# Attention output in the model dimension's own order, and w_in read in rows of 128 partitions behind unit 0's v

## The chip, the cores and the metric

The kernel runs on one core of one Trainium2 chip. The metric is the device time of one execution in microseconds, as the median over several runs of the whole kernel; less is better.

## What is computed

Per batch and head a gated recurrence over 768 steps gives an attention output; the heads are laid side by side (8 heads of 48, 384 in all) and go through a two-layer block whose activation is a rational function.

```python
# q, k, v, f_logit: [4, 8, 768, 48]
f = 1 / (1 + exp(-f_logit))
for t in range(768):
    state = f[:, :, t, :, None] * state + k[:, :, t, :, None] * v[:, :, t, None, :]
    y[:, :, t] = q[:, :, t] @ state
x = y, heads side by side            # [3072, 384]
h = x @ w_in                         # [384, 2048]
P = a0 + a1*h + a2*h**2 + a3*h**3
Q = 1 + |b0| * |h| + |b1| * h**2
out = (P / (Q + 1e-6)) @ w_out       # [2048, 384]
```

## The kernel before

The work is cut into 12 units of 256 tokens: unit n is batch n mod 4 and chunk n div 4, so a state is handed on from unit n to unit n + 4. Within a unit the heads go in four pairs (index a), and the tokens in two blocks j of 128.

The order of every instruction is written out by hand in the string ORDER (lines 19 to 100). A loop at the end calls one small function for each step; each engine then takes its own steps in that order and waits only for data, for buffers and for PSUM slots. There are four PSUM slots; "@1" behind a step names its slot. A step therefore waits for everything that stands before it on its own engine, and for the last reader of its slot.

The steps that matter here:

- ld n f, k, q (line 190): loads of 384 KB (or halves of 192 KB) on SP's DMA queue, with three buffers for each of them. ld n v goes on POOL's queue, since it casts to bf16.
- wi m0 m1 (load_w_in, lines 193 to 200): w_in's columns m0*128 to m1*128, cast to bf16, on POOL's queue. The contracted dimension of 384 lies in three groups kk of 128 partitions. One transfer is issued for each kk, and partition 32a + e of group kk holds row 96a + 32kk + e. The order issues "wi 4 16" right behind unit 0's first loads, and "wi 0 4" later, with no wait before it on POOL.
- vm n x (line 349): POOL copies parts of v together for the heads' middle piece; it waits for v.
- ci: POOL makes the identity matrix that the transposes need; cu and cm make the triangular matrices and the mask.
- ef, ls, cs, A: ACT takes exp and log of the gate, PE sums it along time (cs), ACT takes exp of the sums (A). xa (DVE, line 296): products of q and k with A. T (PE, line 312) transposes them, Te copies them out, sc (PE, line 334) makes the scores, mk (DVE, line 342) masks them.
- yb and yi (line 355, through ymm): the attention output, from the scores and from the carried state. They write 32 columns of a pair's 96 at a time; piece kk of pair a goes to partitions 32a to 32a + 31 and to column block kk of the PSUM tile, which is why w_in has the row order above. ye (ACT, line 411) copies it to xT. sv and st renew the state.
- h n m0 m1 (PE, line 432): x times w_in, four blocks of 128 columns; hy (ACT) copies it out. h n 12 16 is each unit's first or one of its first; unit 0 takes 12 16, then 8 12, 4 8 and 0 4.
- sq, ab, u, ln, lz, zd, p1, p2, pm, ta, ex, gm: the rational function on DVE, ACT and PE, where zd and ta are accumulating transfers of 512 KB on POOL's queue. o (PE, line 539) multiplies by w_out, oe and so bring it out.

In PE's order, unit 0's y and unit 1's transpose T 1 stand ahead of unit 0's first h; yb 0 uses slot 1, which cs 1 used before it.

Of the kernel before, what the change touches and what calls it, by code (L numbers as in the profile page):

```python
# [17 lines left out]

ORDER = """
cz 0; ab_ b a; ld 0 f 2 4; ld 0 v; ld 0 f 0 2; cz 3; cu 1; ld 0 k 0 2; cz 1; cu 0; ld 0 q 2 4; fa  # L20
ld 0 q 0 2; wi 4 16; ef 0 2 4; ld 0 k 2 4; cz 2; ef 0 0 2; ls 0 0 2; fr; ls 0 2 4; cs 0 2 4 @1; vm 0 1
ld 1 f; cs 0 0 2 @0; ld 1 v; A 0 1 0 2; A 0 1 2 4; xa 0 1 0 2; A 0 0 2 4; vm 0 0; A 0 0 0 2; ci; xa 0 0 2 4
ld 1 k; xa 0 0 0 2; xa 0 1 2 4; T 0 0 2 @2; T 0 2 4 @1; Te 0 0 2; Te 0 2 4; sc 0 0 @2; ld 1 q; sv 0 0 @0
ef 1; cm; sc 0 1 @3; mk 0 0; ls 1; ae 0; cs 1 @1; ab_ a s; mk 0 1; A 1 1; st 0 0; A 1 0; xa 1 1; sv 0 1
yb 0 0 2 @1; ld 2 f; yi 0 1; xa 1 0; yb 0 2 4; ld 2 q; wi 0 4; ye 0 s; fb; T 1 @3; st 0 1; h 0 12 16 @0
# [83 lines left out]
def kernel(  # L109
# [12 lines left out]
    nc = tc.nc  # L122
    B, H, S, D = q.shape
    C = 128
    P = 128
    HP = H // 2
    DM = H * D
    d_ff = moe_w_in.shape[1]
    KD = DM // P
# [11 lines left out]
    ld = ctx.enter_context(tc.tile_pool(name="ld", bufs=3))  # L141
# [22 lines left out]
    w_in_sb = consts.tile([P, KD, d_ff], BF16, name="w_in_sb")  # L164
# [26 lines left out]
                      in_=src[s["b"], hh, t0:t0 + NT, :].rearrange("h (p i) d -> p h (i d)", i=2))  # L191

    def load_w_in(m0, m1):

        n = (m1 - m0) * P
        for kk in range(KD):
            nc.gpsimd.dma_start(out=w_in_sb[:, kk, m0 * P:m1 * P],
                                in_=bass.AP(tensor=moe_w_in.tensor,
                                            offset=moe_w_in.offset + 32 * kk * d_ff + m0 * P,
                                            ap=[[96 * d_ff, HP], [d_ff, 32], [1, n]]))  # L200

    def load_w_out(m0, m1):
        nc.gpsimd.dma_start(out=w_out_sb[:, m0:m1, :],
# [148 lines left out]
    PIECE = ((0, 0), (0, 1), (1, 1), (1, 2))  # L352

    def ymm(s, j, a, kk, lhsT, rhs):
        nc.tensor.matmul(s["y"][32 * a:32 * a + 32, j, kk * C:kk * C + C].rearrange("e (i t) -> e i t", i=2),  # L355
                         lhsT, rhs, start=(j, a) not in s["begun"], stop=True, skip_group_check=True)
        s["begun"].add((j, a))

    def y_open(s, sl):
        if "y" not in s:  # L360
# [3 lines left out]
    def yi(n, j, sl=None):  # L364
        s = unit(n)
        y_open(s, sl)
        for kk in range(KD):
            for a in range(HP):
                ymm(s, j, a, kk, s["st"][j][:, a, 32 * kk:32 * kk + 32], s["T"][:, 0, :, a, R * j:R * j + R])

    def yb(n, a0=0, a1=HP, sl=None):
        s = unit(n)
        y_open(s, sl)
        for i0 in range(2):
            for par, kk in PIECE:
                for a in range(a0, a1):
                    for j in range(UB):
                        r = slice(R * j, R * j + R)
                        if kk == 1:
                            w = s["vm"][r, i0, a, 16 * par:16 * par + 32]  # L380
                        else:
                            w = s["v"][r, 2 * a + par, i0, 16 * par:16 * par + 32]
                        ymm(s, j, a, kk, w,
                            s["scm", a // 2][r, 2 * par + a % 2, i0 * C:i0 * C + C].rearrange("s (i t) -> s i t", i=2))
# [171 lines left out]
    def behind(i, mark):  # L556
        tc.add_manual_dep(i.ins, marks[mark].ins.name,
                          mybir.DependencyInfo(mybir.DependencyClass.Sync, mybir.DependencyReason.DATA),
                          reason="begins behind it")

    steps = dict(ld=load, wi=load_w_in, wo=load_w_out, ab_=load_ab, cu=const_u, ci=const_i, cm=const_m,
                 cz=const_z, fa=coef_a, fb=coef_b, fr=coef_r, ef=ef, ls=ls, cs=cs, A=A, xa=xa, T=T, Te=Te,
                 sc=sc, mk=mk, vm=vm, yi=yi, yb=yb, sv=sv, ye=ye, ae=ae, st=st, h=h, hy=hy, sq=sq, ab=ab, u=u, ln=ln,
# [38 lines left out]
```

## Time and profile before

| | |
|---|---|
| Runs shown | 247.44, 248.99, 253.96 us (median 248.99) |
| Span of the profiled execution | 247.6 us; the page gives no other time of it |
| Busy, share of the span | PE 88%, DVE 83%, ACT 77%, POOL 26%, PE weight loads 61% |
| TensorE clock granted | full in all slices |
| DMA queues, share of 16 engines | POOL's 61.6%, SP's 33.2% |
| First matmul of h | 30.5 us |
| w_in | 6 issues, 13.1 to 16.3 us from issue to landing |

A timeline row reads: start, length, engine, line, operation, out<-in, shape and count, and in brackets how long the engine had idled before it and what ended that. A row of the chain that ended last has start, length and what the end hung on. A row of DMA issues has the tensor, the queue, the count, the size of one and the median us from issue to landing. Rows that begin with q0 or q1 give a queue's packets, MB and the share that they took of 16 engines in the window that was asked for.

### The profile page before, as it was taken

The numbers are of one execution on the slowest core, as the hardware profiler recorded it, in microseconds if no ns is written. First come the engines' busy times: TensorE is split into PE (matmuls) and PEld (weight loads), VectorE is DVE, ScalarE is ACT, GpSimd is POOL, SyncE is SP. The second block draws the span as 40 slices with busy tenths as digits, with TensorE's granted clock in tenths as the row PEclk, the third lists the DMA queues.
The fourth block names the chain that finished last, engine by engine and source line by source line (L and its number), as shares of the span: only waits on it lengthen the run. The fifth ranks groups of instructions, "written<-read, shape, count | busy, mean of one in ns | idle before, by whom it ended". The sixth has DMA issues, their size and how long they took to land.

```text
span 247.6 us, 7084 instructions
## 1 busy us (share of the span) xinstructions
PE 216.8 (88%) x3128; PEld 151.8 (61%) x3128; DVE 205.9 (83%) x232; ACT 190.4 (77%) x197; POOL 64.4 (26%) x94
## 2 busy tenths in 40 slices
PE   0307898979899998989999999999999999999990
PEld 0204676667557675756767776656866867664550
DVE  5217568999998969979979999999899898999630
ACT  3402376998995986996988998997965997799961
POOL 7421004233022400543042144202203311133200
PEclk9999999999999999999999999999999999999999
DMA  7999999995979899999896998799934996389954
GB/s 116 203 188 177 199 221 263 195 173 91 160 140 165 196 225 238 233 243 178 210 225 106 179 259 175 141 200 281 203 36 88 164 208 132 77 159 197 176 116 128
DMA packets 64206, 43.72 MB, mean 177 GB/s; under 512 B 53680, under 2 KB 59184, under 8 KB 64176
## 3 DMA queue, kind: packets, MB, share of 16 engines
q0 software_dynamic: 22944, 24.39, 61.6%
q1 hardware_dynamic: 41088, 18.88, 33.2%
q8 instruction: 24, 0.39, 0.6%
q14 instruction: 6, 0.05, 0.0%
q10 hardware_dynamic: 144, 0.00, 0.0%
HBM read 25.17 MB, written 4.72 MB: 121 GB/s over the span
## 4 chain that ended last, share of the span: by engine, by line
PE 64%; DMA 11%; ACT 11%; issue 7%; DVE 3%; SPq 2%; ACTq 0%; POOLq 0%
PE hp L432 21%; PE op L539 17%; DMA fn<-in_f_logit_dram 7%; PE y L355 7%; PE u L466 5%; PE tp L312 4%; DMA gall<-hy 4%; PE cs L282 3%; PE sc L334 3%; ACT lq L491 2%; PE sv L403 2%; ACT qi L499 2%; ACT hy L446 2%; ACT lq L477 2%; SPq L190 2%
## 5 line engine op out<-in xcount | busy, mean ns | idle before, releaser
L539 PE MATMUL op<-w_out_sb,gall 128*128 128x384 bf16 x384 | 69.4, 327 | 2.8 <-issue 1.0
L432 PE MATMUL hp<-xT,w_in_sb 128*128 128x256 bf16 x576 | 69.5, 274 | 1.1 <-ACT xT L411 0.9
L432 PEld LDWEIGHTS <-w_in_sb 128*128 128x128 bf16 x576 | 55.5, 98 | 12.0 <-issue 1.5
L446 ACT CAST hy<-hp 128x1024 bf16<-128x1024 f32 x48 | 47.9, 1017 | 11.4 <-PE hp L432 11.2
L539 PEld LDWEIGHTS <-gall 128*128 128x128 bf16 x384 | 35.7, 98 | 28.0 <-issue 2.8
L499 ACT ACTIVATE qi<-lq 128x2048 bf16<-128x2048 f32 x24 | 45.9, 1919 | 0.2
L522 POOL DMA_DIRECT2D gall<-hy x24 | 22.4, 962 | 72.4 <-DVE gall L518 24.5
L486 POOL DMA_DIRECT2D z<-h x12 | 13.2, 1099 | 76.8 <-DVE z L458 29.5
L342 DVE TENSOR_TENSOR scm<-sc,mask 128x1024 bf16<-128x1024 f32 x24 | 29.0, 1219 | 4.5 <-PE sc L334 4.3
L531 DVE TENSOR_TENSOR gall<-gall,qi 128x2048 bf16<-128x2048 bf16 x24 | 29.2, 1219 | 4.2 <-DMA gall<-hy 2.4
L450 DVE TENSOR_TENSOR h<-hy 128x2048 bf16<-128x2048 bf16 x24 | 29.1, 1217 | 0.4 <-ACT hy L446 0.4
L518 DVE TENSOR_TENSOR gall<-gall,h 128x2048 bf16<-128x2048 bf16 x24 | 28.9, 1217 | 0.0
L477 ACT ACTIVATE lq<-u 128x1024 f32<-128x1024 f32 x24 | 24.1, 1031 | 3.1 <-PE u L466 2.9
L291 ACT ACTIVATE A<-cs 128x768 f32<-128x768 f32 (+1 forms) x26 | 18.7, 767 | 6.0 <-PE cs L282 5.8
L491 ACT ACTIVATE lq<-z 128x2048 f32<-128x2048 bf16 x12 | 23.1, 1921 | 0.0
L296 DVE TENSOR_TENSOR qkp<-kn,A 128x768 bf16<-128x768 f32 (+1 forms) x13 | 11.7, 900 | 13.2 <-DMA kn<-in_k_dram 7.9
L267 ACT ACTIVATE fn<-fn 128x768 f32<-128x768 f32 (+1 forms) x13 | 10.3, 799 | 15.7 <-DMA fn<-in_f_logit_dram 15.7
L312 PE MATMUL tp<-ident,qkp 128*128 128x128 bf16 x192 | 14.6, 235 | 8.3 <-DVE qkp L296 5.6
L282 PE MATMUL cs<-lsp,Ui 128*128 128x384 bf16 (+1 forms) x39 | 10.9, 346 | 9.3 <-ACT lsp L272 9.3
L320 DVE COPY qkT<-tp 128x2048 bf16<-128x2048 bf16 (+1 forms) x13 | 14.8, 1138 | 5.1 <-PE tp L312 3.0
L312 PEld LDWEIGHTS <-qkp 128*128 128x128 bf16 x192 | 12.5, 105 | 10.1 <-DVE qkp L296 7.5
L349 POOL COPY vmp<-vn 128x128 bf16<-128x128 bf16 x24 | 12.6, 603 | 18.0 <-DMA vn<-in_v_dram 18.0
(63 smaller groups left out, 286.3 us busy)
## 6 DMA issues: line engine op xcount, KB each, us to landing
gall<-hy POOLq DMA_DIRECT2D x24, 512.0 KB, 6.7
z<-h POOLq DMA_DIRECT2D x12, 512.0 KB, 6.5
out_dram<-osb SPq DMA_DIRECT2D x24, 192.0 KB, 4.1
fn<-in_f_logit_dram SPq DMA_DIRECT2D x11, 384.0 KB, 10.3
kn<-in_k_dram SPq DMA_DIRECT2D x11, 384.0 KB, 6.1
qn<-in_q_dram SPq DMA_DIRECT2D x11, 384.0 KB, 8.1
vn<-in_v_dram POOLq DMA_DIRECT2D x12, 192.0 KB, 8.6
w_out_sb<-in_moe_w_out_dram POOLq DMA_DIRECT2D x4, 384.0 KB, 9.7
```

What stands on the lines that cost most here:

```text
L312: nc.tensor.transpose(t[:, x, i, p, :], s["qk"][:, x, i, 2 * p:2 * p + 2, :].rearrange("t h d -> t (h d)"), ident)
L342: return nc.vector.tensor_mul(t, s["sc", g].rearrange("s r a i t -> s (r a) (i t)"), mb)
L432: nc.tensor.matmul(t[:, m - m0, :].rearrange("f (j t) -> f j t", j=UB), w_in_sb[:, kk, m * P:(m + 1) * P], s["x"][:, :, kk, :], start=(kk ...
L446: nc.scalar.copy(fl(big(s, "hy", "hy", 3), m0, m1), fl(s["hp", m0], 0, m1 - m0))
L450: return nc.vector.tensor_mul(fl(big(s, "h2", "h2", 2), m0, m1), fl(s["hy"], m0, m1), fl(s["hy"], m0, m1))
L477: nc.scalar.activation(fl(lq(s, g), m0 - 8 * g, m1 - 8 * g), fl(s["u", m0], 0, m1 - m0), AF.Ln, scale=regs[2], bias=1.0 + 1e-6)
L491: nc.scalar.activation(fl(lq(s, g), m0 - 8 * g, m1 - 8 * g), fl(s["z"], m0, m1), AF.Ln, scale=regs[2], bias=1.0 + 1e-6)
L499: nc.scalar.activation(fl(s["qi", g], m0 - 8 * g, m1 - 8 * g), fl(s["lq", g], m0 - 8 * g, m1 - 8 * g), AF.Exp, scale=-1.0)
L518: return nc.vector.tensor_mul(fl(s["g"], m0, m1), fl(s["g"], m0, m1), fl(s["h2"], m0, m1))
L522: nc.gpsimd.dma_start(out=fl(s["g"], m0, m1), in_=fl(s["hy"], m0, m1), accum_op=ALU.add)
L531: return nc.vector.tensor_mul(fl(s["g"], m0, m1), fl(s["g"], m0, m1), fl(s["qi", g], m0 - 8 * g, m1 - 8 * g))
L539: nc.tensor.matmul(s["op"][:, j, 0:DM], s["g"][:, m, C * j:C * j + C], w_out_sb[:, m, :], start=(s["on", j] == 1), stop=(s["on", j] == KF))
```

## The change

Three things are changed together. First, ymm no longer places piece kk of pair a by (a, kk) but by the number 3a + kk, which is the piece's place in the model dimension: block (3a + kk) div 4, partitions 32 * ((3a + kk) mod 4) and on. Partition p of block b now holds row 128b + p of the model dimension.

Second, load_w_in reads plain rows: partition p of group kk is row 128kk + p, and one transfer carries all three groups.

Third, in the order "wi 4 16" is split into "wi 8 16" and "wi 4 8", and both go behind the two vm steps of unit 0, so behind the landing of its v; "wi 8 16" comes ahead of unit 1's v and "wi 4 8" behind it. ci goes ahead of the vm steps. "wi 0 4" stays in its place in the text, which on POOL is now right behind "wi 4 8".

```diff
-ld 0 q 0 2; wi 4 16; ef 0 2 4; ld 0 k 2 4; cz 2; ef 0 0 2; ls 0 0 2; fr; ls 0 2 4; cs 0 2 4 @1; vm 0 1
-ld 1 f; cs 0 0 2 @0; ld 1 v; A 0 1 0 2; A 0 1 2 4; xa 0 1 0 2; A 0 0 2 4; vm 0 0; A 0 0 0 2; ci; xa 0 0 2 4
+ld 0 q 0 2; ef 0 2 4; ld 0 k 2 4; cz 2; ef 0 0 2; ls 0 0 2; fr; ls 0 2 4; ci; cs 0 2 4 @1; vm 0 1
+ld 1 f; cs 0 0 2 @0; A 0 1 0 2; A 0 1 2 4; xa 0 1 0 2; A 0 0 2 4; vm 0 0; wi 8 16; ld 1 v; A 0 0 0 2; wi 4 8; xa 0 0 2 4
...
     def load_w_in(m0, m1):
-
-        n = (m1 - m0) * P
-        for kk in range(KD):
-            nc.gpsimd.dma_start(out=w_in_sb[:, kk, m0 * P:m1 * P],
-                                in_=bass.AP(tensor=moe_w_in.tensor,
-                                            offset=moe_w_in.offset + 32 * kk * d_ff + m0 * P,
-                                            ap=[[96 * d_ff, HP], [d_ff, 32], [1, n]]))
+        nc.gpsimd.dma_start(out=w_in_sb[:, :, m0 * P:m1 * P],
+                            in_=moe_w_in[:, m0 * P:m1 * P].rearrange("(kk p) n -> p kk n", p=P))
...
     def ymm(s, j, a, kk, lhsT, rhs):
-        nc.tensor.matmul(s["y"][32 * a:32 * a + 32, j, kk * C:kk * C + C].rearrange("e (i t) -> e i t", i=2),
-                         lhsT, rhs, start=(j, a) not in s["begun"], stop=True, skip_group_check=True)
-        s["begun"].add((j, a))
+        blk, qd = divmod(KD * a + kk, 4)
+        nc.tensor.matmul(s["y"][32 * qd:32 * qd + 32, j, blk * C:blk * C + C].rearrange("e (i t) -> e i t", i=2),
+                         lhsT, rhs, start=(j, qd) not in s["begun"], stop=True, skip_group_check=True)
+        s["begun"].add((j, qd))
```

## The prediction

> **What bounds the kernel now.** I read the page's head first, then the busy time of each engine in stretches of 10 us, then the chain that ended last.
>
> ```profile
> span 247.6 us, 7084 instructions
> PE 216.8 (88%) x3128; PEld 151.8 (61%) x3128; DVE 205.9 (83%) x232; ACT 190.4 (77%) x197; POOL 64.4 (26%) x94
> ...
> 10.00:20.00 10.00, 2.63 (x33) 2.10 (x34) 3.19 (x6) 0.79 (x3) 3.57 (x7) 1.00 1.31 175
> 30.00:40.00 10.00, 10.00 (x162) 7.38 (x161) 7.25 (x8) 5.68 (x8) 1.55 (x3) 1.00 1.03 232
> 50.00:60.00 10.00, 8.51 (x190) 7.05 (x190) 9.93 (x12) 9.22 (x12) 2.39 (x5) 1.00 0.83 134
> 90.00:100.00 10.00, 9.19 (x145) 6.94 (x134) 9.45 (x11) 7.37 (x8) 0.77 (x2) 1.00 1.18 235
> 130.00:140.00 10.00, 10.00 (x123) 7.33 (x122) 10.00 (x10) 9.14 (x11) 2.45 (x5) 1.00 0.79 131
> ```
>
> The first columns after the stretch are the busy time of PE, PEld, DVE, ACT and POOL; the last three are clock, DMA share and GB/s. From 30 us on PE, or DVE with ACT, is full in each stretch. Between 10 and 20 us no engine is half busy and DMA is over 1: the start is bound by loads, the rest by engines. Time saved before 30 us should therefore move all that follows. The chain says which load:
>
> ```profile
> 4.93 16.54 DMA fn<-in_f_logit_dram
> 21.50 0.85 ACT fn L267
> 22.37 0.85 ACT lsp L272
> 23.27 1.45 PE cs L282 x4
> 24.74 1.52 ACT A L291 x2
> 26.30 2.46 PE y L355 x75
> 30.58 2.13 PE hp L432 x12
> ```
>
> Unit 1's f is issued at 4.93 and lands at 21.47. Its ef, ls, cs and A follow without a gap, and unit 0's y must wait for A because it takes the PSUM slot that cs held. Unit 1's f alone is not enough to cure, since other loads are nearly as late:
>
> ```profile
> 5.54 7.33 SPq L190 DMA_DIRECT2D kn<-in_k_dram  x1
> 17.77 0.56 DVE L296 TENSOR_TENSOR qkp<-kn,A 128x384 bf16<-128x384 f32 x1 [6.20 <-DMA kn<-in_k_dram]
> 20.79 2.36 DVE L342 TENSOR_TENSOR scm<-sc,mask 128x1024 bf16<-128x1024 f32 x2
> 20.94 0.66 PE L334 MATMUL sc<-qkT 48*64 48x128 bf16 x14
> 28.32 0.96 DVE L296 TENSOR_TENSOR qkp<-qn,A 128x768 bf16<-128x768 f32 x1 [1.78 <-DMA qn<-in_q_dram]
> 33.66 0.85 ACT L267 ACTIVATE fn<-fn 128x768 f32<-128x768 f32 x1
> ```
>
> The second half of unit 0's k holds DVE until 17.77 and with it the scores. Unit 1's q holds it until 28.32; its transpose T 1 stands in PE's order ahead of the first h, at 30.58. SP needs 7.33 us to issue one load because its queue is full.
>
> **What w_in does to these loads.** Issues, landings (the last number, us from issue) and what the queues moved, q0 being POOL's and q1 SP's; the first "DMA packets" row is of 4 to 7 us, the next of 7 to 11, then q0 of 11 to 16, q0 and q1 of 12 to 15, q1 of 20 to 28:
>
> ```profile
> 4.16 2.04 POOL L197 DMA_DIRECT2D w_in_sb<-in_moe_w_in_dram  x3
> 9.66 0.29 POOL L349 COPY vmp<-vn 128x128 bf16<-128x128 bf16 x1 [3.46 <-DMA vn<-in_v_dram]
> 11.66 1.99 POOL L197 DMA_DIRECT2D w_in_sb<-in_moe_w_in_dram  x3
> ...
> w_in_sb<-in_moe_w_in_dram POOLq DMA_DIRECT2D x1, 384.0 KB, 13.1
> w_in_sb<-in_moe_w_in_dram POOLq DMA_DIRECT2D x2, 384.0 KB, 15.4
> w_in_sb<-in_moe_w_in_dram POOLq DMA_DIRECT2D x2, 128.0 KB, 15.9
> vn<-in_v_dram POOLq DMA_DIRECT2D x1, 192.0 KB, 8.3
> fn<-in_f_logit_dram SPq DMA_DIRECT2D x1, 384.0 KB, 9.4
> ...
> DMA packets 2169, 0.63 MB, mean 210 GB/s; under 512 B 2169, under 2 KB 2169, under 8 KB 2169
> DMA packets 2330, 0.83 MB, mean 208 GB/s; under 512 B 2257, under 2 KB 2257, under 8 KB 2330
> q0 software_dynamic: 782, 0.84, 118.0%
> q0 software_dynamic: 477, 0.53, 132.2%
> q1 hardware_dynamic: 122, 0.05, 9.2%
> q1 hardware_dynamic: 3012, 1.09, 74.0%
> ```
>
> Before 7 us every packet is small, though w_in was issued from 4.16 on: 2.8 us pass before its large packets come. Then SP's queue falls to 122 packets in 3 us (41 per us), against 377 per us between 20 and 28, when only v and narrow w_in rows run beside it. That is the wait of the start.
>
> **The change, part by part.**
>
> 1. w_in leaves the place ahead of unit 0's v. It is now issued behind both vmp copies, which wait for v at 9.66, or a little sooner without w_in beside it. The issue falls at about 9.0 to 10.2, its packets run from 11.8 to 13.0. Until then SP's loads and v are alone. A 384 KB load is 1024 packets (128 partitions, 8 heads), so unit 0's f, k, q, v and unit 1's f are 5120. At 580 (2330 in 4 us) to 720 packets per us (2169 in 3), from 2.3 us and with 1.3 us to the semaphore, unit 1's f lands at 10.7 to 12.4 instead of 21.47, and unit 0's last k before it, under 11 instead of 17.7.
>
> 2. First chain: DVE's k product follows its q products at 11.6 instead of 17.77, 6.2 earlier, so both score products (20.79 + 2.36) end at 16.9 and the state product behind them under 1 us later. Second chain: f at 12.0, then ef and ls, 1.7; cs waits on PE behind unit 0's last scores, which end at 21.6 and now at 15.4; then 1.45 and 1.52 give 18.4. Unit 0's y begins at 18.4 instead of 26.30, and h by that chain at 18.4 + 4.3 = 22.7.
>
> 3. Unit 1's q: 7168 packets in all (six loads and v). By 12.4, about the middle of the start of w_in, 5900 or more are done. The 8..16 part is 768 KB; q0 moved 0.84 MB in 5 us, so it takes 4.7 us, in which SP gets about 41 per us, 190. The other 1080 at 377 per us take 2.9 us. Landing: 12.4 + 4.7 + 2.9 + 1.3 = 21.3. Ends: 14.5, if it gets through ahead of w_in, and 25, if SP stays at 41 per us for the second w_in part too. I take 20.9, nearer the middle, as f and k may run at 720. From q to h is 30.58 - 28.32 = 2.3: h begins at 23.2, so this wait ends last. Gain 7.4 us; ends 3.3 and 7.9.
>
> 4. w_in itself: 8..16 lands near 18.5, and h 0 12 16 and h 0 8 12 need it at 23.2. Its two other parts come behind v of unit 1 and are 384 KB each, 2.3 us at the same pace, more beside SP: about 24.5 and 27.5; h wants them at 27.4 and 30.8. Cost nothing; cover lost, it is time for time.
>
> 5. Next late: unit 2's f. It landed at 30.6 (21.20 + 9.4) and ef used it at 33.66, three us of slack. Now it follows q by the same 2.4 us plus what w_in takes, 23 to 28, and ef wants it at 26.3. Between 0 and 1.7 us; I take 0.7.
>
> 6. Later loads come 2 to 3 us earlier and engines 7, so DMA slack shrinks. One transfer stood in the chain already and DVE waited on two loads:
>
> ```profile
> 83.79 9.09 DMA gall<-hy
> 88.33 0.96 DVE L296 TENSOR_TENSOR qkp<-kn,A 128x768 bf16<-128x768 f32 x1 [1.66 <-DMA kn<-in_k_dram]
> 92.91 1.23 DVE gall L531
> ```
>
> Between 0 and 4 us (the difference of 7 and 3); I take 1.2, since 50 to 60 has a DMA share of 0.83 to catch up in.
>
> 7. POOL: six issues of 0.68 become three of about 0.7 to 1, and ident is made before the wait for v. POOL idles 3.46 us at 9.66; nothing on the path. The v of unit 1 is issued behind one w_in part, a microsecond or two later than 9.89, and is wanted after 30.
>
> 8. The column quarters that y writes. Rows of one y pass:
>
> ```profile
> 55.00 0.28 PE L355 MATMUL y<-scm,vmp 64*32 64x128 bf16 x8
> 55.11 0.28 PE L355 MATMUL y<-scm,vn 64*32 64x128 bf16 x8
> ```
>
> Eight matmuls in 0.11 us, four to each 55 ns: two row halves by two column quarters run together, and the next four use the same quarters. The new quarter is (3a + kk) mod 4: for a = 0, 1 the pieces take 0,3 then 1,0 then 1,0 then 2,1. The busiest quarter is used three times in four pieces, not four, so a half pass takes at best 333 of 444 ns. 24 half passes: 0 to 2.6 us less; PE is full for about half of them, so I take 1.0. y from the state keeps four quarters to a round: nothing.
>
> Sum: 247.6 - 7.4 + 0.7 + 1.2 - 1.0 = 241.1. The page has no other time for that execution; its span lies 0.2 above the fastest run shown (247.44) and 1.4 under the median (248.99). Half that distance added, the forecast is 242.0.
>
> **A page against the trace.** The Trainium skill, "DMA: Bandwidth & Descriptors", section "Why a DMA increments its semaphore by 16 and not by 1", says that a transfer is spread over the largest number of engines up to 16 that divides the slowest dimension on both sides. By it w_in's old source (4 by 32 rows) sat on 4 engines and three transfers on 12, the new one on all 16, and the busiest engine's w_in would fall from 128 KB to 96 KB. No row here shows engines one by one, so the sum leaves it out; by it an estimated 1 to 2 us more would be won.
>
> **The rivals.**
>
> A. The collision only moves: w_in falls on unit 1's k and q on all engines alike, q lands at 25 and h begins at 27.3. For it: 41 packets per us between 12 and 15. Against: 377 later. Gain 3.3 + 1.0 - 1.2, so 244.5 in span and 245.4 as a time. The same page, section "Queues, rings and completion order", has the engines take turns between queues; the row agrees, and by that rule this rival is what happens if POOL's queue never runs empty.
>
> B. The start is won and given back by 110 us, as accumulating transfers and loads collide (step 6 at its far end, 4, and f at 1.7): 247.6 - 7.4 + 5.7 - 0.6 = 245.3, time 246.2. Against: PE, not DMA, is full from 110 us on.
>
> C. Slower: w_in comes after the attention. If 8..16 moves like two old 384 KB transfers end to end (13.1 to 15.4 each) from 8.6, it lands at 34.8 to 39.4, and h, PE's next work, waits for it: 4.2 to 8.8 us later than 30.58, so 252 to 256. It decides once 8..16 lands after 30.58. Against: the old six shared those us with each other.
>
> D. Nothing changes at the start: unit 1's f stays near 21 because total traffic is the same. Then only step 8: 247 to 249. Against: the order in each queue decides, and 41 per us is w_in's doing.
>
> **How the numbers follow.** Forecast 0.56, A 0.18, B 0.12, C 0.07, D 0.07. Two per cent, about what a measurement of this kernel can tell from no change, is 244.0 against 248.99. The forecast's own range is 238.5 to 244.5 (below: q at 14.5, 0.5 more, step 8 in full, 1.6 more, and step 6 at nothing, 1.2 more; above: f and step 6 at 4.4 together). To leave out no more than 2 in 10 the range goes on to 248.5, over A, B and most of D. Faster: most of the forecast and a little of A, 0.57; same: the rest of it, A, B, D, 0.33; slower: C and scatter, 0.10.
>
> **What would show it.** Right: ACT's ef of unit 1 near 12 and not 21.5; DVE's second k product near 11.6; y near 18.4; first h near 23 with its idle time ended by q, not by w_in; yb half passes under 0.4 us. Wrong: first h after 27 (A), a wait on w_in in PE's list (C), more DMA-ended idle time on DVE and ACT between 40 and 110 (B).

## Result and the profile after

The changed kernel takes 239.11 us in the median of four runs (238.29 to 240.47), the kernel before 248.48 us beside it: the ratio is 0.962, with a 95% interval of 0.956 to 0.968. Five undisturbed runs in a later series gave 238.26 to 240.15. The forecast of 242.0 had the direction and most of the size; its explanation was only half right, as the experiments show. In the stretches below the columns are as in the prediction.

The head of the page after, with POOL's queue, and two stretches of the busy times:

```profile
span 238.8 us, 7065 instructions
PE 213.7 (89%) x3113; PEld 148.6 (62%) x3128; DVE 206.0 (86%) x232; ACT 190.6 (80%) x197; POOL 61.7 (26%) x91
q0 software_dynamic: 20976, 24.38, 62.6%
...
10.00:20.00 10.00, 8.62 (x172) 5.59 (x171) 7.44 (x14) 3.74 (x7) 3.37 (x5) 1.00 1.09 194
30.00:40.00 10.00, 8.93 (x129) 6.61 (x128) 9.72 (x11) 8.77 (x11) 3.22 (x5) 1.00 1.18 220
```

PE is at work for 8.62 us between 10 and 20, where it had 2.63. The work itself is nearly unchanged (PE 213.7 against 216.8 us, DVE and ACT alike): the time came out of the idle start. In order of time, from the chain that ended last and from the timeline of DVE, ACT and PE:

```profile
5.45 3.46 SPq L190
8.95 10.77 DMA qn<-in_q_dram
...
11.01 0.55 DVE L291 TENSOR_TENSOR qkp<-kn,A 128x384 bf16<-128x384 f32 x1
12.19 0.84 ACT L262 ACTIVATE fn<-fn 128x768 f32<-128x768 f32 x1 [1.87 <-DMA fn<-in_f_logit_dram]
19.82 0.96 DVE L291 TENSOR_TENSOR qkp<-qn,A 128x768 bf16<-128x768 f32 x1 [1.75 <-DMA qn<-in_q_dram]
22.04 1.47 PE L428 MATMUL hp<-xT,w_in_sb 128*128 128x256 bf16 x12 [0.17 <-DVE state L419]
25.25 0.84 ACT L262 ACTIVATE fn<-fn 128x768 f32<-128x768 f32 x1 [0.69 <-DMA fn<-in_f_logit_dram]
```

Unit 0's last k (the first DVE row) is used at 11.0 instead of 17.8, unit 1's f at 12.2 instead of 21.5, its q at 19.8 instead of 28.3, and h begins at 22.0 instead of 30.6. The load that now stands in the chain is unit 1's q, no longer its f. SP's queue tells why loads come earlier; between 7 and 12 us it moved, before and after,

```profile
q1 hardware_dynamic: 1690, 0.63, 73.0%
...
q1 hardware_dynamic: 3290, 1.24, 105.9%
```

twice the packets. In the packed trace, which has the start of every packet and every change of the granted clock, the first large row of w_in starts only at 12.2.

### The profile page after: what moved, and what is told of

The parts are those of the page before. It is cut to its first block, busy times and chain, and to the rows that moved or that the text cites. A ratio compares the mean times of both kernels' runs of the same rounds, so it can differ in the third digit from the quotient of the medians.

```text
span 238.8 us, 7065 instructions
## 1 busy us (share of the span) xinstructions
PE 213.7 (89%) x3113; PEld 148.6 (62%) x3128; DVE 206.0 (86%) x232; ACT 190.6 (80%) x197; POOL 61.7 (26%) x91
## 3 DMA queue, kind: packets, MB, share of 16 engines
q0 software_dynamic: 20976, 24.38, 62.6%
## 4 chain that ended last, share of the span: by engine, by line
PE 63%; ACT 10%; DMA 10%; issue 7%; DVE 4%; SPq 4%; ACTq 0%; DVEq 0%; POOLq 0%
PE hp L428 22%; PE op L535 18%; PE u L462 6%; PE y L351 5%; DMA qn<-in_q_dram 5%; DMA gall<-hy 4%; PE tp L307 4%; SPq L190 3%; PE sc L329 3%; ACT qi L495 2%; PE cs L277 2%; ACT lq L487 2%; PE sv L399 2%; ACT hy L442 2%; ACT lq L473 2%
## 5 line engine op out<-in xcount | busy, mean ns | idle before, releaser
L428 PE MATMUL hp<-xT,w_in_sb 128*128 128x256 bf16 x576 | 68.6, 273 | 1.1 <-ACT xT L407 0.9
L442 ACT CAST hy<-hp 128x1024 bf16<-128x1024 f32 x48 | 47.8, 1016 | 10.7 <-PE hp L428 10.4
L518 POOL DMA_DIRECT2D gall<-hy x24 | 22.4, 962 | 71.5 <-DVE gall L514 19.7
L407 ACT ACTIVATE xT<-y 128x768 bf16<-128x768 f32 x12 | 9.7, 812 | 9.6 <-PE y L351 9.6
L454 DVE TENSOR_SCALAR z<-hy 128x2048 uint16<-128x2048 uint16 x24 | 16.8, 711 | 0.0
L344 POOL COPY vmp<-vn 128x128 bf16<-128x128 bf16 x24 | 11.8, 572 | 19.3 <-DMA vn<-in_v_dram 19.3
L505 DVE TENSOR_SCALAR hy<-hy,a_sb 128x4096 bf16<-128x4096 bf16 x12 | 16.6, 1384 | 0.0
```

Source lines behind the costliest of these rows:

```text
L428: nc.tensor.matmul(t[:, m - m0, :].rearrange("f (j t) -> f j t", j=UB), w_in_sb[:, kk, m * P:(m + 1) * P], s["x"][:, :, kk, :], start=(kk ...
L442: nc.scalar.copy(fl(big(s, "hy", "hy", 3), m0, m1), fl(s["hp", m0], 0, m1 - m0))
L518: nc.gpsimd.dma_start(out=fl(s["g"], m0, m1), in_=fl(s["hy"], m0, m1), accum_op=ALU.add)
```

## The experiments

Two theories stood against each other. The order theory is the prediction's: w_in simply came too early and stopped SP's loads. The spread theory: w_in's old source, 4 blocks of 32 rows that do not join in memory, kept each transfer on few DMA engines, and the plain rows cured that. y's new columns are a third, small part. In four of the kernels (old columns beside plain rows, columns alone, 8 and 2 blocks) the rows that meet in h are not the reference's pairs, so their output is another; the work is the same. Ratios are to the kernel before in the same series, with 95% intervals.

| Kernel | us | Ratio |
|---|---|---|
| New order alone | 247.70 | 0.995 (0.991 to 0.999) |
| New rows and columns, old order | 243.14 | 0.972 (0.965 to 0.979) |
| All but the columns | 240.14 | 0.966 (0.961 to 0.971) |
| All, w_in's first part halved | 239.17 | 0.959 (0.955 to 0.964) |
| All, again | 239.08 | 0.960 (0.954 to 0.965) |
| All, three transfers a part | 238.95 | 0.961 (0.952 to 0.969) |
| All, source written as 4 blocks that join | 238.39 | 0.957 (0.950 to 0.963) |
| All, 8 blocks of 16 rows | 240.16 | 0.958 (0.950 to 0.965) |
| All, 2 blocks of 64 rows | 252.04 | 1.010 (1.006 to 1.015) |
| Columns alone | 247.20 | 0.993 (0.989 to 0.997) |

**The order alone.** The diff is that of ORDER; load_w_in keeps its three transfers a part and ymm its columns.

> The kernel before with only the order changed (w_in in three parts behind unit 0's v, ci early); rows, three transfers a part and y's columns as before. Theory (the order makes the start): w_in's large packets begin near 12, unit 1's f lands at 11 to 12, its q at 20.6, as an engine that holds w_in holds a little more of it; h begins at 23, time 241.5 us. Rival (the spread of w_in over all engines makes the start): q lands after 24, h begins after 26, 244.5 us or more.

It gave 247.7 us. Neither expectation holds as a whole. The start is as the order theory says: unit 1's q is used at 20.97 and h begins at 23.19. Then it is lost again. From the timelines of DVE, PE and POOL, the chain, POOL's queue on the page and one stretch of busy times:

```profile
20.97 0.96 DVE L296 TENSOR_TENSOR qkp<-qn,A 128x768 bf16<-128x768 f32 x1 [2.90 <-DMA qn<-in_q_dram]
...
23.19 1.47 PE L432 MATMUL hp<-xT,w_in_sb 128*128 128x256 bf16 x12 [0.59 <-DVE state L423]
29.56 0.28 PE L432 MATMUL hp<-xT,w_in_sb 128*128 128x256 bf16 x1 [2.42 <-DMA w_in_sb<-in_moe_w_in_dram]
35.17 1.76 PE L432 MATMUL hp<-xT,w_in_sb 128*128 128x256 bf16 x12
...
20.73 0.66 POOL L197 DMA_DIRECT2D w_in_sb<-in_moe_w_in_dram  x1 [5.20 <-DMA w_in_sb<-in_moe_w_in_dram]
...
22.09 13.52 DMA w_in_sb<-in_moe_w_in_dram
...
q0 software_dynamic: 24528, 24.40, 61.9%
...
32.00:34.00 2.00, 2.00 (x30) 1.25 (x28) 0.00 (x0) 1.01 (x1) 1.01 (x2) 0.50 1.39 210
```

The third h waits for w_in and the fourth begins at 35.17, where the changed kernel has it at 29.3. POOL must wait 5.2 us for an earlier w_in transfer before it may issue the next, and the last one, issued at 22.09, takes 13.5 us for 128 KB. That is rival C of the prediction, w_in after the attention, in a part of the change. The stall costs more than the wait: behind it the granted TensorE clock is 0.50 (the third number from the end of the last row), in the packed trace from 31.4 to 34.8 us.

**The rows and columns, in the old order.** ORDER as before, load_w_in and ymm new.

> The changed kernel with the old order (w_in 4 to 16 behind unit 0's first loads, 0 to 4 late): plain rows, one transfer a part and the new columns alone. Theory (the order makes the start): SP's loads still stand still for 6 us from 7 or 8 us on; unit 0's last k lands near 14, unit 1's f at 16, its q at 26, h begins at 28.5; with 1.5 us from y's columns 245 us. Rival (the spread over engines makes it): f at 12 to 13, q near 21, h at 23.5, 240 us.

243.1 us, between the two theories. From DVE's, ACT's and PE's timelines:

```profile
12.77 0.56 DVE L291 TENSOR_TENSOR qkp<-kn,A 128x384 bf16<-128x384 f32 x1 [1.63 <-DMA kn<-in_k_dram]
17.75 0.84 ACT L262 ACTIVATE fn<-fn 128x768 f32<-128x768 f32 x1 [7.28 <-DMA fn<-in_f_logit_dram]
26.21 2.53 PE L428 MATMUL hp<-xT,w_in_sb 128*128 128x256 bf16 x12
```

f is held back by w_in and lands some 5.6 us later than in the changed kernel, as the order theory says, but 3.7 us earlier than before with w_in in the very same place. Plain rows in one transfer a part do not hold the loads up as long.

Two kernels of the table have the new order and y's old columns: "New order alone" and "All but the columns". They differ only in w_in's rows and the count of its transfers, and have 0.995 against 0.966.

**What the blocks do.** Three kernels have the new order and columns and three transfers a part, so nine like the order alone, and differ in the blocks of the source alone:

```diff
-        nc.gpsimd.dma_start(out=w_in_sb[:, :, m0 * P:m1 * P],
-                            in_=moe_w_in[:, m0 * P:m1 * P].rearrange("(kk p) n -> p kk n", p=P))
+        for kk in range(KD):
+            nc.gpsimd.dma_start(out=w_in_sb[:, kk, m0 * P:m1 * P],
+                                in_=moe_w_in[kk * P:(kk + 1) * P, m0 * P:m1 * P])
...
# 8 blocks: in_ = AP(offset + 16*kk*d_ff + m0*P, [[48*d_ff, 8], [d_ff, 16], [1, n]])
# 2 blocks: in_ = AP(offset + 64*kk*d_ff + m0*P, [[192*d_ff, 2], [d_ff, 64], [1, n]])
```

> The changed kernel with plain rows, but three transfers a part, one for each group of 128 rows: nine transfers as in the order alone, each with 128 rows outermost as in the changed kernel. Theory (the old source of 4 by 32 rows keeps a transfer on few engines, and this is what made the order alone fail): w_in 8 to 16 lands by 20, the last part by 28, though POOL must wait with its last two issues for a free semaphore; no wait on w_in in PE, 239.5 us. Rival (nine transfers in eight semaphores made it fail): POOL's wait of 5 us returns, the third and fourth h wait for w_in until 30 and after, 243 us or more.

> The changed kernel with three transfers a part whose source is 8 blocks of 16 rows, 48 rows apart, so that the blocks do not join in memory; the rows that meet in h are not the reference's pairs. Theory (the outermost count of the source sets the number of engines): 8 engines hold a transfer, 16 packets each; POOL's queue counts 21072 + 9 x 8 x 16 = 22224 packets; w_in 8 to 16 is 5.5 us on the busier eight engines, first h near 22.5, no later wait on w_in: 239 to 240.5 us. Rival (spread is even, the number of blocks is without effect): 21072 packets, 239.0 us; or (any split into blocks costs what the order alone lost): 245 us or more.

> The same with 2 blocks of 64 rows, 192 rows apart; the rows that meet in h are not the reference's pairs. Theory: 2 engines hold a transfer, 64 packets each; POOL's queue counts 21072 + 9 x 14 x 64 = 29136 packets; 8 to 16 takes 11 us on its engines, with SP's between near 13, and lands at about 26; POOL's last two issues wait for it, the last part lands at 35 or later; first h at 26 to 28, third or fourth waits for w_in: 246 to 250 us. Rival (the number of blocks is without effect): 21072 packets, 239.0 us.

The count of transfers is not it: nine transfers of plain rows took 238.95 us. POOL waited there too, but shortly, and the fourth h began without a wait at 29.06:

```profile
q0 software_dynamic: 21072, 24.38, 62.8%
...
15.74 0.53 POOL L195 DMA_DIRECT2D w_in_sb<-in_moe_w_in_dram  x1 [1.97 <-DMA w_in_sb<-in_moe_w_in_dram]
29.06 1.48 PE L429 MATMUL hp<-xT,w_in_sb 128*128 128x256 bf16 x12
```

The number of blocks is what matters, as 2 blocks show, and the packet counts follow it. With 8 blocks, POOL's queue and the third h:

```profile
q0 software_dynamic: 22224, 24.39, 62.8%
27.27 1.26 PE L431 MATMUL hp<-xT,w_in_sb 128*128 128x256 bf16 x10 [0.42 <-DMA w_in_sb<-in_moe_w_in_dram]
```

With 2 blocks, POOL's queue, the first h and the next issue of POOL:

```profile
q0 software_dynamic: 29136, 24.42, 61.8%
25.66 0.39 PE L431 MATMUL hp<-xT,w_in_sb 128*128 128x256 bf16 x1 [4.56 <-DMA w_in_sb<-in_moe_w_in_dram]
25.90 0.78 POOL L195 DMA_DIRECT2D w_in_sb<-in_moe_w_in_dram  x1 [10.52 <-DMA w_in_sb<-in_moe_w_in_dram]
```

Both packet counts are those expected to the last packet. The times are less so. With 8 blocks the first h came sooner than expected (21.48), but the third and fourth waited 1.0 us for w_in, where no wait was expected. With 2 blocks the time is 2 us over the expected range. There the first four h waited 12.2 us for w_in up to 45 us, and the clock was 0.50 in the packed trace from 23.9 to 34.1 and from 40.9 to 47.8; how the loss divides between the waits and the clock was not measured.

The counts fit one rule, inferred from the kernel before and the order alone and then forecast for 8 and 2 blocks: a transfer of b blocks runs on b of the 16 engines, 128/b rows on each, and each idle engine is given as many packets of its own, which carry next to nothing (the queue's MB stay the same, and the added packets are of 4 bytes each in the packed trace). 8 blocks: 9 transfers by 8 idle engines by 16 rows, 1152 more than 21072. 2 blocks: 9 by 14 by 64, 8064 more. The same rule gives the kernel before (6 transfers of 4 blocks, 6 x 12 x 32 = 2304 more) its 22944 packets against 20976 after, since it has 384 fewer data packets and, at 16 for a transfer, 48 more completion packets; and it gives the order alone its 24528. (The 16 are read from three transfers a part: 6 transfers and 96 packets more than the changed kernel.) No row shows the engines one by one, so the rule is shown by its counts. They agree with what the Trainium skill, "DMA: Bandwidth & Descriptors", section "Why a DMA increments its semaphore by 16 and not by 1", says of the number of engines. In time, as ratios to the kernel before: 1.010 for 2 blocks, 0.995 for 4 (with the old columns, about 0.007 of it), 0.958 for 8 and 0.961 for none; the last two cannot be told apart.

**Blocks that join in memory.** One transfer a part with the source written as 4 by 32 by 3 rows, where the 4 blocks follow one another.

> The changed kernel with one transfer a part, its source written as 4 by 32 rows by 3 groups: three transfers, the same rows and bytes, only the outermost count on the source side is 4 again. Theory (a transfer runs on as many engines as divide the outermost counts, here 4): 384 large packets on four engines are 96 each, 16.5 us at 172 ns besides SP's; 8 to 16 lands near 32, the first h waits for it, unit 1's q near 25; 249 to 251 us, slower than the kernel before or the same. Rival (how the source is written does not matter): as the changed kernel, 239.1 us.

```profile
q0 software_dynamic: 20976, 24.38, 62.4%
```

238.4 us (ratio 0.957, 0.950 to 0.963) and the packet count of the changed kernel: 4 blocks of 32 rows without a gap are 128 rows again. This run is a miss as a test of the rule, and a second copy of the changed kernel. One transfer a part with gaps between the blocks, so on 4 engines, was not measured; three transfers against one were compared for plain rows alone.

**The columns.** ymm back as before, in the changed kernel; and the new ymm alone in the kernel before.

```diff
-        blk, qd = divmod(KD * a + kk, 4)
-        nc.tensor.matmul(s["y"][32 * qd:32 * qd + 32, j, blk * C:blk * C + C].rearrange("e (i t) -> e i t", i=2),
+        nc.tensor.matmul(s["y"][32 * a:32 * a + 32, j, kk * C:kk * C + C].rearrange("e (i t) -> e i t", i=2),
```

> The changed kernel with one part undone: y's pieces go back to column quarter a (old ymm), while w_in keeps its plain rows, so the rows that meet in h are not the reference's pairs. Theory (the new quarters save PE time): a half pass of y in the later units takes 0.44 us to its last start again instead of about 0.35; h begins at 22.0 as in the changed kernel, but from 110 us on, where PE is full, some 1.5 us are lost over seven units: 240.6 us, shift against the kernel before falling back to about 7.3 us at the end. Rival (matmuls on different quarters gain nothing, the end shift of 8.8 is the start's alone): 239.1 us.

> The kernel before with only y's new column quarters; w_in's rows and order as before, so the rows that meet in h are not the reference's pairs. Theory (busiest quarter three uses in four, not four): start as before, h at 30.5; from the time PE is full the shift grows by 1.0 to 1.5 us to the end: 247.5 us. Rival (the columns give nothing): 248.8 us, no growth of the shift.

Alone the columns gave 0.993, 1.8 us (0.8 to 2.8); undone they cost about 1 us (240.1 against 239.1, in different series), but those two intervals overlap. The traces are clearer. A half pass of y before (its first rows, and y from the state right behind), then after:

```profile
71.59 0.24 PE L355 MATMUL y<-scm,vn 64*32 64x128 bf16 x4
71.66 0.28 PE L355 MATMUL y<-scm,vmp 64*32 64x128 bf16 x8
...
72.15 0.35 PE L355 MATMUL y<-qkT,state 128*32 128x128 bf16 x12
...
63.67 0.24 PE L351 MATMUL y<-scm,vn 64*32 64x128 bf16 x4
63.69 0.23 PE L351 MATMUL y<-scm,vmp 64*32 64x128 bf16 x2
64.12 0.35 PE L351 MATMUL y<-qkT,state 128*32 128x128 bf16 x12
```

Up to the rows from the state, 0.56 us became 0.45, and the second piece starts 0.02 us behind the first instead of 0.07. With the old columns in the changed kernel it is 0.56 again (62.99 to 63.55). Whether that reaches the end is read from when xT is copied in unit 6 (a group row, whose start stands behind the comma) and in unit 11 (a timeline row): before, after, and with the old columns.

```profile
L411 ACT ACTIVATE xT<-y x1: 810/810/810, 130.0 to 130.0; 128x768 bf16<-128x768 f32 x1
212.03 0.81 ACT L411 ACTIVATE xT<-y 128x768 bf16<-128x768 f32 x1 [2.25 <-PE y L355]
...
L407 ACT ACTIVATE xT<-y x1: 811/811/811, 122.5 to 122.5; 128x768 bf16<-128x768 f32 x1
203.22 0.81 ACT L407 ACTIVATE xT<-y 128x768 bf16<-128x768 f32 x1 [2.05 <-PE y L351]
...
L406 ACT ACTIVATE xT<-y x1: 810/810/810, 121.3 to 121.3; 128x768 bf16<-128x768 f32 x1
202.96 0.81 ACT L406 ACTIVATE xT<-y 128x768 bf16<-128x768 f32 x1 [2.25 <-PE y L350]
```

From unit 6 to unit 11, with PE full, the changed kernel's lead grows from 7.5 to 8.8 us, that of the old columns from 8.7 to 9.1. One trace of each would be little, as unit 6 itself moves by more than 1 us from trace to trace. But the time from unit 6's copy to unit 11's is 82.0, 81.7 and 81.7 us in the three traces with old columns (before, order alone, all but the columns). Of the nine traces with new columns, eight have 80.7 to 80.9 and one 82.0. The new columns bring 0.8 to 1.3 us in these units.

**A smaller first part.** "wi 8 16" split into "wi 12 16" ahead of unit 1's v and "wi 8 12" behind it.

> The changed kernel with its first w_in part halved: 12 to 16 behind v, then unit 1's v, then 8 to 12, 4 to 8 and 0 to 4. Theory (unit 1's q, held up behind 4.6 us of w_in, sets the first h): 2.3 us of w_in stand ahead of q, the small v packets share evenly, q lands at 17.5 to 18.5 and h begins at 20.8 to 21.2, set by y's chain or by q; 238.2 us. Rival (y's chain or PE sets h already, or the second half comes too late for h 0 8 12): h at 22.0 or a wait on w_in ahead of the second h, 239.1 us or more.

```profile
18.00 0.95 DVE L291 TENSOR_TENSOR qkp<-qn,A 128x768 bf16<-128x768 f32 x1
21.52 2.52 PE L428 MATMUL hp<-xT,w_in_sb 128*128 128x256 bf16 x12
26.66 1.49 PE L428 MATMUL hp<-xT,w_in_sb 128*128 128x256 bf16 x12 [0.50 <-DMA w_in_sb<-in_moe_w_in_dram]
```

q is ready at 18.0 without a wait, as expected, but h begins only 0.5 us earlier, behind y, takes 2.52 us instead of 1.47, and the third h waits for w_in: 239.2 us, no gain. The rival was right in the time, though the wait on w_in came one block later than it said. No version here beats the changed kernel by more than the scatter.

**Once more.** The changed kernel beside the blocks:

> The changed kernel once more, beside the others of this call and to compare with the old columns: 239.1 us.

239.08 us.

## Why the prediction was right, and where it was not

- Step 1 and step 2 hold: f was used at 12.2 (landing at 10.7 to 12.4 forecast), the second k product began at 11.0 (11.6), y at 17.8 (18.4). No row shows the 1.3 us from the last packet to the semaphore that both landings count; the runs show the landings alone.
- Step 3 holds in mechanism, and unit 1's q is the load in the chain; it landed at 19.7 instead of 20.9, and h began 8.5 us earlier instead of 7.4. The term was 1.1 us too small. For the order alone it was nearly exact (q used at 20.97, h at 23.19, 23.2 forecast), so the rest seems to go with the plain rows.
- Step 4 reached the right number for the changed kernel, but named the wrong cover. "Cost nothing" was credited to the order and to the pace of POOL's queue. The order alone, with w_in on 4 engines a transfer by the rule above, failed there: w_in came late and took back most of what it had won. Even with plain rows the cover was thin: the second part landed at 25.2 (24.5 forecast) and the third h began at 25.55, so 0.4 us were left where the forecast had 2.9. The spread over all engines, which the prediction kept out of its sum as an estimated 1 to 2 us, is what the step stands on. That the number came out is partly luck. By the ratios, the order alone brings 0.5%, rows and columns without the order 2.8%, all together 4.0% (the repeated run). The order alone keeps little of what it wins, and the rows bring most of their gain without it. Whether the two together bring more than their sum, the intervals do not tell.
- The sentence "41 per us is w_in's doing" is right, but not by w_in's place alone: with the same place and plain rows f landed 3.7 us earlier.
- Step 5: ACT waited 0.69 us for unit 2's f; 0.7 was forecast, taken from between 0 and 1.7.
- Step 6 is not shown. In this trace the lead fell from 8.9 us at unit 0's xT to 7.5 at unit 6, step 5's wait included, where steps 5 and 6 had 1.9. In the trace of the joined blocks, a second copy of the kernel, it was 9.7 at unit 6. The waits of DVE and ACT on DMA between 40 and 110 us are 4.3 us in all, before and after. The accumulating transfer that stood in the chain before stands there still, as long as before, and ACT waits for a gate load behind it:

```profile
75.79 9.18 DMA gall<-hy
88.13 0.84 ACT L262 ACTIVATE fn<-fn 128x768 f32<-128x768 f32 x1 [2.05 <-DMA fn<-in_f_logit_dram]
```

- Step 8: 1.0 us forecast; 0.8 to 1.3 by the traces from unit 6 on, 1 to 1.8 by the times of the whole kernel. A half pass became 0.11 us shorter, which is the step's best case (333 of 444 ns).
- A term that the sum did not have: the twelve matmuls of the first h took 2.17 us before and 1.47 after, so 0.7 us of lead came with the clock (last section). Nothing in the prediction foresaw it.
- From span to time the prediction added 0.9 us. In every run on record the time is about 1.7 us above the span (240.47 against 238.8). In spans the miss is 2.3 us, 241.1 against 238.8, and not the 2.9 of 242.0 against 239.11. The lower end of the forecast's own range is 238.7 by its own terms, not 238.5.

Rival A (q at 25) and D (f near 21) did not come. B's sign, more idle time that DMA ends on DVE and ACT, did not come either. C came, but only where the source was left in blocks.

## What to carry to other kernels

Before a transfer is moved later, look at how many engines it runs on: a source that is cut into b blocks with gaps between them counts like b engines here, and its landing, not its bytes, decides whether it may be late. The packet count of a queue gives the number away, since by the rule above idle engines get packets too. When a change has two parts, test each alone: here the order brought 0.5%, rows and columns 2.8%, and all together 4.0%.

## What the runs showed of the hardware that was not expected

- POOL's packets count the engines that a transfer leaves idle, by the rule above: 22944 before, 20976 after, 24528, 22224 and 29136 in the experiments, all by one formula.
- The same twelve matmuls of the first h took 1.47 us in the changed kernel and 2.52 with the smaller first part, at a granted clock that the view reads as full in both. The Trainium skill, "TensorE: Matmul & The Clock Gate", part 1 on the clock gate, has the array at half speed until it has been busy for a free-running window of about 3.4 us. The traces agree. With 2 blocks, where the view has the clock at 0.50, twelve matmuls took 2.48 us:

```profile
32.00:34.00 2.00, 2.00 (x14) 1.41 (x11) 1.22 (x1) 1.97 (x3) 0.67 (x1) 0.50 1.06 206
32.03 2.48 PE L431 MATMUL hp<-xT,w_in_sb 128*128 128x256 bf16 x12
```

The packed trace's list of granted clocks has no entry ahead of the first full one, and the view reads full there. That entry stands at 21.9 us in the changed kernel, ahead of its first h at 22.04, and at 23.7 with the smaller first part, behind its first h at 21.52. Before the change it stands at 32.0, behind the first h at 30.55, which took 2.17 us; so "full in all slices" does not hold ahead of 32 us. Inside the runs the stretches at 0.50 last 3.4 us (31.4 to 34.8 in the order alone) or two or three times that. The half speed cost the smaller first part the microsecond that its earlier load had won.
